# Rows of an expert past 768 as a branched tail of a mixture-of-experts kernel

## The chip, the cores and the metric

The kernel runs on one core of one Trainium2 chip. The metric is the device time of one execution in microseconds (us): median of 3 runs before the change 1105.15 us (1104.6 to 1109.25). The input is drawn with a fixed seed, so each run routes the same tokens to the same experts.

## The reference

```python
x = attn_ref(q, k, v, alpha)        # gated linear attention, (3072 tokens, 384)
logits = x @ w_gate                 # 8 experts
noisy = logits + np.log1p(np.exp(x @ w_noise)) * noise
top2 = np.argpartition(-noisy, 2, axis=1)[:, :2]
w = softmax of the two chosen noisy logits
for e in range(8):                  # tokens that chose e
    h = np.maximum(x[mask] @ w1[e], 0.0)          # 384 -> 1024
    out[mask] += w[mask, k, None] * (h @ w2[e])   # 1024 -> 384
return ((out @ w_a) * (out @ w_b)) @ w_out        # 384 -> 1536 -> 384
```

Each token goes to two experts, so 6144 rows are shared by 8 experts, 768 on average. Counted from the reference on its fixed input, the experts 0 to 7 get 748, 771, 773, 759, 762, 760, 749 and 822 rows.

## The kernel before

TensorE (PE) does everything in full precision by splitting each float32 operand into a high and a low part (`split`, L106) and adding three products (`prod3`, L629 to L631): high by high, high by low, low by high. Each of the three is one weight load (LDWEIGHTS, row PEld) and one matmul (row PE).

The program is written out by hand, in order, engine by engine. After the attention (to about 154 us) the experts follow one another. Expert e has a fixed number of row places: `CAP` = 832 for experts 1 to 6, and `ROWS` = 896 for experts 0 and 7 (`rows_of`). Experts 0 and 7 are "parted": rows of the first 14 token tiles lie in the first `CAPA` = 512 places, the others start at place 512, with a gap between where the first group has fewer. For expert 0 this lets the first part begin before the routing of the last tiles is known, for expert 7 it lets the last layer gather its first rows early. Rows past the capacity set a flag, and a slow path at the end (`tc.If(over > 0)`, L914) computes everything again; on this input it is not taken.

An expert is an up stage and a down stage. In the up stage (`up_unit`), for each of 8 slices f of the hidden dimension, 9 matmuls (3 slices of 384 inputs by 3 products) stream the rows as columns: experts 1 to 6 in two halves of 416 columns, so 8 x 2 x 9 = 144 matmuls; expert 7 in parts of 512 and 384 columns, 72 matmuls each. ScalarE (ACT) and VectorE (DVE) then write the high and low part of the result to `HB` (L646, L647). In the down stage (`down_unit`), each of 7 tiles of 128 rows takes 24 matmuls of 384 columns; the last tile of an expert with 832 places overlaps the tile before it and writes 64 rows. ACT copies the result out (L663), and a DMA puts it into the table `y2` in device memory.

Beside this, ACT and POOL split the next weights (`w_split`, L108, L109), POOL gathers the next expert's rows, PE transposes them (`x_unit`, L370) and ACT and DVE split them (L372, L373). In expert 7, `gather2` fetches rows of `y2` for the last layer, `x2_sum` adds the two experts of a token, and `x2_unit` transposes the sum; `split_more` splits the last layer's weights. In the last layer (`up2_unit`, `down2_unit`) no row count enters.

`nc.values_load` (L816) reads the flag into a register of every engine, after expert 0. The Exp and Ln of the routing (L232, L237, L344) make ACT load function tables in between.

Of the kernel before, what the change touches and what calls it, by code (L numbers as in the profile page):

```python
# [7 lines left out]
F32 = mybir.dt.float32  # L8
# [13 lines left out]
DM = H * D  # L22
KD = DM // 128
E = 8
# [6 lines left out]
CAPA, CAPB = 512, 384  # L31
CAP = 832
ROWS = CAPA + CAPB
NJ = 7
# [13 lines left out]
def parted(e):  # L48
    return e in (0, E - 1)

# [10 lines left out]
def moe_kernel(ctx: ExitStack, tc, qka0, qka1, afirst, v, wgn, noise, w1, w2, w3, out):  # L61
# [14 lines left out]
    xd = tc.dram_tile([N, DM], F32, name="xd")  # L76
    total = base_of(E - 1) + ROWS
    y2 = tc.dram_tile([total, DM], F32, name="y2")
# [19 lines left out]
    idx = tl(const, [128, E * NJ], I32, "idx")  # L98
    flag = tl(const, [1, 1], I32, "flag")

    sctx = ctx.enter_context(ExitStack())
# [76 lines left out]
    def route_consts():  # L178
        nc.sync.dma_start(wgn_t, wgn)
        nc.sync.dma_start(noise_t, noise)  # L180
        iota(e4096, [[4096, E]])
        iota(prio, [[-1, E]], base=E)
        iota(keys.rearrange("p (e j) -> p e j", e=E), [[32, E], [1, NJ]])
        iota(lane, [[1, 128]])
        iota(token, [[128, NT]], base=-1024, channel=1)
        nc.gpsimd.memset(lacc, 1024.0)
        nc.gpsimd.memset(least, 0.0)
        nc.gpsimd.memset(least[:, ::E - 1], CAPA / 128)
        nc.gpsimd.memset(room[:, 0], float(N))
        nc.gpsimd.memset(room[:, 0, ::E - 1], float(CAPA))  # L190
        nc.gpsimd.memset(room[:, 1], float(CAP))
        nc.gpsimd.memset(room[:, 1, ::E - 1], float(ROWS))
        for n, t in d0.items():
            nc.gpsimd.memset(t, 1.0)
            nc.gpsimd.memset(t[:, :, 0:1], 0.0)
# [16 lines left out]
    def route(g):  # L212
# [77 lines left out]
        if half:  # L290
            nc.vector.tensor_tensor(counts[:, int(last)], pc, room[:, int(last)], op=ALU.is_gt)
            if not last:
                carry[0] = tl(rt, [128, E], F32, "carry")
# [39 lines left out]
    def weights():  # L333
# [6 lines left out]
        nc.vector.tensor_tensor(rf, rf, ri, op=ALU.add)  # L340
        nc.vector.tensor_scalar(row[:, :SPLIT], rf[:, :SPLIT], float(total - CAPB - 1), None, op0=ALU.min)
        nc.vector.tensor_scalar(row[:, SPLIT:], rf[:, SPLIT:], float(total - 1), None, op0=ALU.min)
# [292 lines left out]
    def up_unit(e, f, cols):  # L635

        for s0, n in cols:
# [11 lines left out]
            tick()  # L649

    def down_unit(e, j, mid={}):
        c0 = min(128 * j, rows_of(e) - 128)
# [111 lines left out]
    def gather2(i):  # L764
        g = []
        for k in range(2):
            t = tl(rows, [128, DM], F32, "row")
            src = y2[:total - CAPB] if i < SPLIT else y2
            nc.gpsimd.indirect_dma_start(out=t, out_offset=None, in_=src,  # L769
# [38 lines left out]
    for j in range(NA, NJ):  # L808
# [6 lines left out]
        bg()  # L815
    over = nc.values_load(flag[0:1, 0:1], min_val=0, max_val=1)  # L816
    for e in range(1, E - 1):
        for f in range(NF1):
            up_unit(e, f, [(0, CAP // 2), (CAP // 2, CAP // 2)])
            if f < NJ:  # L820
                gather(e + 1, f)
            w_split()
            w_load()
            bg()
        for j in range(NJ):
            x_unit(e + 1, j)
            down_unit(e, j)
            for _ in range(1 + (j == NJ - 1)):
# [9 lines left out]
    for f in range(NF1):  # L838
        up_unit(e, f, parts[0])
        w_split()  # L840
# [7 lines left out]
    for f in range(NF1):  # L848
        up_unit(e, f, parts[1])
        if f < NFREE:  # L850
            split_more()
    for j in range(TB):
        x2_sum(j)
    for j in range(NA, NJ):
        n = j - NA
        down_unit(e, j, {f: (lambda q=q: x2_unit(q)) for f, q in (((5, 0),), ((3, 1),), ((1, 2),))[n]})
        for _ in range(4):
            split_more()


# [148 lines left out]
```

## Time and profile before

| | |
|---|---|
| runs (3) | 1104.6, 1105.15, 1109.25 us |
| profiled execution: own time, span of the trace | 1108.54 us, 1106.8 us |
| PE busy, chain of waits | 97% of the span; 92% of the chain |
| granted TensorE clock, mean | 0.979 |
| expert 1 (up from 228.68, down from 256.18) | to 287.99 us |
| expert 7 | 584.45 to 643.99 us |
| last layer | 643.99 us to the end |

The rows of the trace that matter stand in a section of their own below. "Start" is counted from the start of the span. A matmul's own duration (0.33 us and the like) is longer than the distance between two starts, since matmuls are pipelined: what a stretch costs is read from the distance between starts. DVEq, PEldq and the like are an engine's instruction sequencer, which runs ahead of the engine.

### The profile page before, as it was taken

What the parts mean: (1) busy time and instruction counts of PE and PEld (TensorE: products, weight loads), DVE (VectorE), ACT (ScalarE), POOL (GpSimd) and SP (SyncE); (2) the same over time, 40 slices, a digit from 0 to 9 for tenths busy, and PEclk for the clock granted to TensorE, in tenths of its full rate; (3) what the DMA queues carried; (4) which work ended last, traced back from release to release, by engine and by line L of the source; (5) the groups of instructions that cost most, each with busy time, mean ns of one, the idle gap of its engine ahead of it and who ended that gap; (6) DMA issues with size and microseconds to landing.
All of it is one profiled execution on the core that took longest, in us unless ns stands there. A gap on an engine that the chain in (4) does not pass through costs nothing.

```text
span 1106.8 us, 19015 instructions
## 1 busy us (share of the span) xinstructions
PE 1075.2 (97%) x7482; PEld 1045.3 (94%) x7482; DVE 485.8 (44%) x850; ACT 416.3 (38%) x900; POOL 401.6 (36%) x428
## 2 busy tenths in 40 slices
PE   7997997999999999999999999999999999999998
PEld 5996877899999999999998999999999999999997
DVE  8988847554443536262622364231314141414130
ACT  2454252454444444443533454232323231313131
POOL 5785523475655546473734364010101010100000
PEclk9998598999999999999999999999999999999999
DMA  8999022563544454454523363011111101010000
GB/s 283 241 234 217 32 78 81 172 201 120 161 132 153 146 163 137 132 161 129 187 89 97 108 194 106 23 30 35 30 37 29 36 22 44 22 36 1 22 1 24
DMA packets 62861, 114.71 MB, mean 104 GB/s; under 512 B 8528, under 2 KB 50352, under 8 KB 62768
## 3 DMA queue, kind: packets, MB, share of 16 engines
q1 hardware_dynamic: 56208, 93.59, 28.2%
q0 software_dynamic: 6560, 19.86, 6.2%
q8 instruction: 61, 1.00, 0.4%
q14 instruction: 32, 0.26, 0.1%
HBM read 86.48 MB, written 26.94 MB: 102 GB/s over the span
## 4 chain that ended last, share of the span: by engine, by line
PE 92%; DVE 5%; issue 1%; POOL 1%; ACT 1%; DMA 0%; SPq 0%; DVEq 0%; POOLq 0%; ACTq 0%
PE bank L629 27%; PE bank L630 27%; PE bank L631 27%; PE bank L370 2%; PE bank L484 2%; PE bank L508 2%; PE bank L500 1%; PE bank L476 1%; PE bank L531 1%; DVE D L454 1%; DVE A L458 1%; PE bank L564 1%; PE bank L445 1%; DVE at L315 1%; PE bank L553 0%
## 5 line engine op out<-in xcount | busy, mean ns | idle before, releaser
L629 PE MATMUL bank<-X,W 128*128 128x384 f32 (+2 forms) x768 | 264.4, 344 | 1.5 <-ACT X L372 1.1
L630 PE MATMUL bank<-X,W 128*128 128x384 f32 (+2 forms) x768 | 264.3, 344 | 0.2 <-DVE X L373 0.2
L631 PE MATMUL bank<-X,W 128*128 128x384 f32 (+2 forms) x768 | 264.1, 344 | 0.0
L109 POOL TENSOR_TENSOR W<-wst,W 128x384 fp32r<-128x384 f32 x136 | 139.3, 1028 | 177.3 <-ACT W L108 171.2
L629 PE MATMUL bank<-W,HB 128*128 128x384 f32 x448 | 157.0, 351 | 0.0
L631 PE MATMUL bank<-W,HB 128*128 128x384 f32 x448 | 151.9, 339 | 0.0
L769 POOL DMA_INDIRECT row<-y,row x48 | 46.7, 972 | 289.8 <-DVE row L777 186.1
L630 PE MATMUL bank<-W,HB 128*128 128x384 f32 x448 | 151.8, 339 | 0.0
L629 PEld LDWEIGHTS bank<-X,W 128*128 128x128 f32 x768 | 144.2, 188 | 4.4 <-ACT X L372 1.4
L630 PEld LDWEIGHTS bank<-X,W 128*128 128x128 f32 x768 | 144.2, 188 | 2.9 <-DVE X L373 0.5
L631 PEld LDWEIGHTS bank<-X,W 128*128 128x128 f32 x768 | 144.2, 188 | 2.5
L373 DVE TENSOR_TENSOR X<-bank,X 128x384 fp32r<-128x384 f32 (+1 forms) x80 | 43.2, 542 | 200.6 <-ACT X L372 193.9
L871 DVE TENSOR_TENSOR p<-bank,a 128x384 f32<-128x384 f32 x96 | 53.5, 558 | 162.7 <-PE bank L631 161.6
L647 DVE SCALAR_TENSOR_TENSOR HB<-bank,HB 128x416 fp32r<-128x416 f32 (+2 forms) x128 | 76.3, 597 | 103.3 <-ACT HB L646 98.4
L872 ACT ACTIVATE HB<-p 128x384 fp32r<-128x384 f32 x96 | 50.4, 525 | 156.0 <-DVE p L871 151.5
L646 ACT ACTIVATE HB<-bank 128x416 fp32r<-128x416 f32 (+2 forms) x128 | 67.1, 524 | 95.7 <-PE bank L631 83.9
L663 ACT ACTIVATE o<-bank 128x384 f32<-128x384 f32 (+1 forms) x56 | 27.6, 492 | 156.2 <-PE bank L631 109.5
L629 PEld LDWEIGHTS bank<-W,HB 128*128 128x128 f32 x448 | 84.8, 189 | 0.5
L630 PEld LDWEIGHTS bank<-W,HB 128*128 128x128 f32 x448 | 84.9, 189 | 0.1
L631 PEld LDWEIGHTS bank<-W,HB 128*128 128x128 f32 x448 | 84.6, 189 | 0.0
L629 PE MATMUL bank<-EX,HB 128*128 128x384 f32 x240 | 82.1, 342 | 0.0
L630 PE MATMUL bank<-EX,HB 128*128 128x384 f32 x240 | 80.3, 335 | 0.0
(177 smaller groups left out, 1805.5 us busy)
## 6 DMA issues: line engine op xcount, KB each, us to landing
wst<-w SPq DMA_DIRECT2D x128, 192.0 KB
wd<-w SPq DMA_DIRECT2D x36, 384.0 KB
ring<-qka SPq DMA_DIRECT2D x36, 288.0 KB
y<-o SPq DMA_DIRECT2D x50, 192.0 KB
w3f<-u SPq DMA_DIRECT2D x36, 192.0 KB
wst<-w3f SPq DMA_DIRECT2D x36, 192.0 KB
v<-v SPq DMA_DIRECT2D x24, 192.0 KB
xd<-x SPq DMA_DIRECT2D x24, 192.0 KB
```

The lines of the kernel that those rows point to most:

```text
L109: eng.tensor_tensor(l, raw, h.bitcast(F32), op=ALU.subtract)
L370: nc.tensor.transpose(pt[:, k * 128:k * 128 + m], t[:m, k * 128:k * 128 + 128], ident[:m, :m])
L373: nc.vector.tensor_tensor(l, ptv, h.bitcast(F32), op=ALU.subtract)
L629: nc.tensor.matmul(ps, ah, bh, start=first, stop=False)
L630: nc.tensor.matmul(ps, ah, bl, start=False, stop=False)
L631: nc.tensor.matmul(ps, al, bh, start=False, stop=last)
L646: nc.scalar.activation(Hh[:, f, s], pu, AF.Relu)
L647: nc.vector.scalar_tensor_tensor(Hl[:, f, s], pu, 0.0, Hh[:, f, s].bitcast(F32), op0=ALU.max, op1=ALU.subtract)
L663: nc.scalar.activation(o[r0:], pd[r0:], AF.Copy)
L769: nc.gpsimd.indirect_dma_start(out=t, out_offset=None, in_=src, in_offset=bass.IndirectOffsetOnAxis(ap=row[:, i, k:k + 1], axis=0))
L871: nc.vector.tensor_tensor(p, ps[1], a, op=ALU.mult)
L872: nc.scalar.activation(Ph[:, f], p, AF.Copy)
```

## The change

Experts 1 to 7 now have 832 places each, with no gap in expert 7 (expert 0 keeps 896). Their up stage streams 768 rows in every case. The last 64 places (768 to 831) become a tail: `up_tail` computes all 8 slices f for these 64 columns in one bank (72 matmuls of 64 columns), and `down_tail` is the old seventh tile of the down stage (24 matmuls). Both sit in a branch on PE alone, on whether the expert has more than 768 rows; in the other case PE does one matmul into the same bank, whose result no row uses. ACT and DVE do their part in both cases, and in both cases the 64 rows are written. VectorE computes the eight truth values (`tails`), and PE loads seven of them into registers right after the flag. In expert 7, `x2_unit(2)` moves from the middle of the last down tile to behind it, and `split_more` is called six times after each of two tiles instead of four times after each of three. One table set that holds both Exp and Ln is loaded at the start.

```diff
@@ -30,6 +30,7 @@
 SPLIT = 14
 CAPA, CAPB = 512, 384
 CAP = 832
+MAIN = 768
 ROWS = CAPA + CAPB
 NJ = 7
 GROUPS = (14, 10)
@@ -46,7 +47,7 @@
 
 
 def parted(e):
-    return e in (0, E - 1)
+    return e == 0
 
 
 def rows_of(e):
@@ -74,7 +75,8 @@
         return tl(psum, [128, 512], F32, f"bank{i}")
 
     xd = tc.dram_tile([N, DM], F32, name="xd")
-    total = base_of(E - 1) + ROWS
+    total = base_of(E - 1) + CAP
+    early = base_of(E - 1) + CAPA
     y2 = tc.dram_tile([total, DM], F32, name="y2")
     wide = w3.dtype != F32
     w3f = tc.dram_tile([128, 3 * NF2 * 384], F32, name="w3f") if wide else None
@@ -97,6 +99,8 @@
     wt = tl(const, [128, NT, 2], F32, "wt")
     idx = tl(const, [128, E * NJ], I32, "idx")
     flag = tl(const, [1, 1], I32, "flag")
+    tails = tl(const, [1, E], I32, "tails")
+    nc.scalar.preload_act_table_set("natural_log_exp_and_others")
 
     sctx = ctx.enter_context(ExitStack())
     wpool = sctx.enter_context(tc.tile_pool(name="wpool", bufs=1))
@@ -185,11 +189,11 @@
         iota(token, [[128, NT]], base=-1024, channel=1)
         nc.gpsimd.memset(lacc, 1024.0)
         nc.gpsimd.memset(least, 0.0)
-        nc.gpsimd.memset(least[:, ::E - 1], CAPA / 128)
+        nc.gpsimd.memset(least[:, 0:1], CAPA / 128)
         nc.gpsimd.memset(room[:, 0], float(N))
         nc.gpsimd.memset(room[:, 0, ::E - 1], float(CAPA))
         nc.gpsimd.memset(room[:, 1], float(CAP))
-        nc.gpsimd.memset(room[:, 1, ::E - 1], float(ROWS))
+        nc.gpsimd.memset(room[:, 1, 0:1], float(ROWS))
         for n, t in d0.items():
             nc.gpsimd.memset(t, 1.0)
             nc.gpsimd.memset(t[:, :, 0:1], 0.0)
@@ -289,7 +293,9 @@
         nc.vector.tensor_tensor(rs, pr, e4096[:, None, :].to_broadcast(sh), op=ALU.add)
         if half:
             nc.vector.tensor_tensor(counts[:, int(last)], pc, room[:, int(last)], op=ALU.is_gt)
-            if not last:
+            if last:
+                nc.vector.tensor_scalar(tails, pc[0:1], float(MAIN), None, op0=ALU.is_gt)
+            else:
                 carry[0] = tl(rt, [128, E], F32, "carry")
                 nc.vector.scalar_tensor_tensor(carry[0], pc, 1 / 128, least, op0=ALU.mult, op1=ALU.max)
         for k in range(2):
@@ -338,7 +344,7 @@
         nc.vector.tensor_scalar(e1, ei, 1.0, float(ROWS - CAP), op0=ALU.min, op1=ALU.mult)
         nc.vector.scalar_tensor_tensor(rf, ei, float(CAP), e1, op0=ALU.mult, op1=ALU.add)
         nc.vector.tensor_tensor(rf, rf, ri, op=ALU.add)
-        nc.vector.tensor_scalar(row[:, :SPLIT], rf[:, :SPLIT], float(total - CAPB - 1), None, op0=ALU.min)
+        nc.vector.tensor_scalar(row[:, :SPLIT], rf[:, :SPLIT], float(early - 1), None, op0=ALU.min)
         nc.vector.tensor_scalar(row[:, SPLIT:], rf[:, SPLIT:], float(total - 1), None, op0=ALU.min)
         yield
         nc.scalar.activation(dm, dm, AF.Exp)
@@ -648,6 +654,37 @@
                                            op0=ALU.max, op1=ALU.subtract)
             tick()
 
+    def up_tail(e):
+
+        s = slice(MAIN, CAP)
+        n = CAP - MAIN
+        pu = bank(2 + upn[0] % 4)[:, :NF1 * n]
+        upn[0] += 1
+        with tc.If(more_rows[e] > 0) as c:
+            for f in range(NF1):
+                for k in range(KD):
+                    ks = slice(k * 128, k * 128 + 128)
+                    prod3(pu[:, f * n:f * n + n], (w1h(f)[:, ks], w1l(f)[:, ks]), (Xh[:, k, s], Xl[:, k, s]),
+                          k == 0, k == KD - 1)
+        with c.Else():
+            nc.tensor.matmul(pu, w1h(0)[:, :128], Xh[:, 0, :NF1 * n], start=True, stop=True)
+        pu = pu.rearrange("p (f n) -> p f n", f=NF1)
+        nc.scalar.activation(Hh[:, :, s], pu, AF.Relu)
+        nc.vector.scalar_tensor_tensor(Hl[:, :, s], pu, 0.0, Hh[:, :, s].bitcast(F32), op0=ALU.max, op1=ALU.subtract)
+
+    def down_tail(e):
+        s = slice(CAP - 128, CAP)
+        pd = bank(6 + MAIN // 128 % 2)[:, :DM]
+        with tc.If(more_rows[e] > 0) as c:
+            for f in range(NF1):
+                prod3(pd, (Hh[:, f, s], Hl[:, f, s]), (w2h(f), w2l(f)), f == 0, f == NF1 - 1)
+        with c.Else():
+            nc.tensor.matmul(pd, Hh[:, 0, s], w2h(0), start=True, stop=True)
+        o = tl(outs, [128, DM], F32, "o")
+        r0 = MAIN - (CAP - 128)
+        nc.scalar.activation(o[r0:], pd[r0:], AF.Copy)
+        nc.sync.dma_start(y2[base_of(e) + MAIN:base_of(e) + CAP], o[r0:])
+
     def down_unit(e, j, mid={}):
         c0 = min(128 * j, rows_of(e) - 128)
         s = slice(c0, c0 + 128)
@@ -765,7 +802,7 @@
         g = []
         for k in range(2):
             t = tl(rows, [128, DM], F32, "row")
-            src = y2[:total - CAPB] if i < SPLIT else y2
+            src = y2[:early] if i < SPLIT else y2
             nc.gpsimd.indirect_dma_start(out=t, out_offset=None, in_=src,
                                          in_offset=bass.IndirectOffsetOnAxis(ap=row[:, i, k:k + 1], axis=0))
             g.append(t)
@@ -814,17 +851,23 @@
             w_load()
         bg()
     over = nc.values_load(flag[0:1, 0:1], min_val=0, max_val=1)
+    more_rows = {e: nc.values_load(tails[0:1, e:e + 1], engines=[mybir.EngineType.PE], min_val=0, max_val=1)
+                 for e in range(1, E)}
     for e in range(1, E - 1):
         for f in range(NF1):
-            up_unit(e, f, [(0, CAP // 2), (CAP // 2, CAP // 2)])
+            up_unit(e, f, [(0, MAIN // 2), (MAIN // 2, MAIN // 2)])
             if f < NJ:
                 gather(e + 1, f)
             w_split()
             w_load()
             bg()
+        up_tail(e)
         for j in range(NJ):
             x_unit(e + 1, j)
-            down_unit(e, j)
+            if j < NJ - 1:
+                down_unit(e, j)
+            else:
+                down_tail(e)
             for _ in range(1 + (j == NJ - 1)):
                 w_split()
                 w_load()
@@ -836,7 +879,7 @@
     EX = tl(epool, [128, (NF2 - 2) * 768], F32R, "EX")
     e = E - 1
     for f in range(NF1):
-        up_unit(e, f, parts[0])
+        up_unit(e, f, [(0, CAPA)])
         w_split()
         w_load()
         if f >= NF1 - 4:
@@ -846,16 +889,19 @@
     for j in range(TB):
         gather2(j)
     for f in range(NF1):
-        up_unit(e, f, parts[1])
+        up_unit(e, f, [(CAPA, MAIN - CAPA)])
         if f < NFREE:
             split_more()
+    up_tail(e)
     for j in range(TB):
         x2_sum(j)
-    for j in range(NA, NJ):
+    for j in range(NA, NJ - 1):
         n = j - NA
-        down_unit(e, j, {f: (lambda q=q: x2_unit(q)) for f, q in (((5, 0),), ((3, 1),), ((1, 2),))[n]})
-        for _ in range(4):
+        down_unit(e, j, {f: (lambda q=q: x2_unit(q)) for f, q in ((), ((1, 0), (5, 1)))[n]})
+        for _ in range(6):
             split_more()
+    down_tail(e)
+    x2_unit(2)
 
 
     def up2_unit(blk, f):
```

TensorE's order before, behind expert 0's last down tile (the names: `W` the split weights, `HB` the hidden rows, `X` the transposed rows, `bank` a PSUM bank; the number at the end is partitions by columns):

```order
L629 MATMUL bank_610_3028<-W_86,HB_2324 128x384
L630 MATMUL bank_610_3028<-W_86,HB_2324 128x384
L631 MATMUL bank_610_3028<-W_86,HB_2324 128x384
L816 TENSOR_LOAD flag_82
L629 MATMUL bank_620_3099<-X_93,W_86 128x416
L630 MATMUL bank_620_3099<-X_93,W_86 128x416
L631 MATMUL bank_620_3099<-X_93,W_86 128x416
```

and now:

```order
L635 MATMUL bank_611_3031<-W_88,HB_2326 128x384
L636 MATMUL bank_611_3031<-W_88,HB_2326 128x384
L637 MATMUL bank_611_3031<-W_88,HB_2326 128x384
L853 TENSOR_LOAD flag_82
L854 TENSOR_LOAD tails_83
L854 ISA x2
...
L635 MATMUL bank_621_3172<-X_95,W_88 128x384
L636 MATMUL bank_621_3172<-X_95,W_88 128x384
L637 MATMUL bank_621_3172<-X_95,W_88 128x384
```

Between the flag's load and the first matmul of expert 1 stand now seven loads of a truth value (the pair of `tails` rows above, seven times), each followed by two register instructions (ISA), and the first matmul has 384 columns instead of 416.

TensorE's order now, around the tail of expert 1's up stage (before, the transposes L370 followed the last matmul of 416 columns at once):

```order
L635 MATMUL bank_660_3428<-X_95,W_88 128x384
L636 MATMUL bank_660_3428<-X_95,W_88 128x384
L637 MATMUL bank_660_3428<-X_95,W_88 128x384
L663 COMPARE_AND_BRANCH
L635 MATMUL bank_663_3449<-X_95,W_88 128x64
L636 MATMUL bank_663_3449<-X_95,W_88 128x64
L637 MATMUL bank_663_3449<-X_95,W_88 128x64
...
L663 UNCONDITIONAL_BRANCH
L670 MATMUL bank_663_3449<-X_95,W_88 128x512
L663 UNCONDITIONAL_BRANCH
L376 MATMUL bank_664_3526<-ident_70,row_3196 128x128 x3
L635 MATMUL bank_665_3532<-W_88,HB_2326 128x384
```

Behind the compare-and-branch stand the 72 matmuls of 64 columns (three shown), a jump over the other case, the one matmul of the other case, and a jump to the transposes of the next expert's first tile. `down_tail` has the same form with 24 matmuls of 384 columns (L678, L682).

TensorE's order now, at the end of expert 7:

```order
L637 MATMUL bank_1181_7661<-W_88,HB_2326 128x384
L678 COMPARE_AND_BRANCH
L635 MATMUL bank_1191_7725<-W_88,HB_2326 128x384
L636 MATMUL bank_1191_7725<-W_88,HB_2326 128x384
L637 MATMUL bank_1191_7725<-W_88,HB_2326 128x384
...
L678 UNCONDITIONAL_BRANCH
L682 MATMUL bank_1191_7725<-W_88,HB_2326 128x384
L678 UNCONDITIONAL_BRANCH
L376 MATMUL bank_1193_7755<-ident_70,row_7404 128x128 x3
L635 MATMUL bank_1194_7761<-X_95,W_88 128x384
L636 MATMUL bank_1194_7761<-X_95,W_88 128x384
```

The transposes of the third tile of the last layer's first block (L376) now stand right before that layer's first matmul, which reads what ACT and DVE make of them; before, they stood between matmuls of the last down tile.

## Rows read from the trace of the kernel before

**Rows 1.** Page, busy time of the engines: share of the span, instructions.

```profile
PE 1075.2 (97%) x7482; PEld 1045.3 (94%) x7482; DVE 485.8 (44%) x850; ACT 416.3 (38%) x900; POOL 401.6 (36%) x428
```

**Rows 2.** Page, chain of waits that ended last, share by engine.

```profile
PE 92%; DVE 5%; issue 1%; POOL 1%; ACT 1%; DMA 0%; SPq 0%; DVEq 0%; POOLq 0%; ACTq 0%
```

**Rows 3.** Timeline of TensorE, starts of expert 1: up, transposes, down (start, duration).

```profile
228.68 0.35 PE L629 MATMUL bank<-X,W 128*128 128x416 f32 x1
...
255.93 0.49 PE L370 MATMUL bank<-ident,row 128*128 128x128 f32 x3
256.18 0.42 PE L629 MATMUL bank<-W,HB 128*128 128x384 f32 x1
```

**Rows 4.** Timeline of TensorE, starts of the parts of expert 7.

```profile
584.45 0.39 PE L629 MATMUL bank<-X,W 128*128 128x512 f32 x1
...
600.81 0.35 PE L629 MATMUL bank<-W,HB 128*128 128x384 f32 x1
...
617.71 0.34 PE L629 MATMUL bank<-X,W 128*128 128x384 f32 x1
...
630.20 0.34 PE L629 MATMUL bank<-W,HB 128*128 128x384 f32 x1
```

**Rows 5.** Timeline of TensorE weight loads behind a transpose.

```profile
216.36 0.19 PEld L629 LDWEIGHTS bank<-W,HB 128*128 128x128 f32 x1
216.47 0.19 PEld L630 LDWEIGHTS bank<-W,HB 128*128 128x128 f32 x1
```

**Rows 6.** Chain of waits in the attention (start, length, what).

```profile
86.06 0.87 PE bank L500 x8
...
88.02 1.07 PE bank L508 x32
```

**Rows 7.** Line L816, the flag: duration min/median/max in ns, start.

```profile
L816 PEldq TENSOR_LOAD <-flag x1: 492/492/492, 226.2 to 226.2; - x1
...
L816 SPq TENSOR_LOAD <-flag x1: 498/498/498, 231.2 to 231.2; - x1
L816 SPq FUSED_REGOPS  x1: 191/191/191, 231.8 to 231.8; - x1
L816 SPq SEQ_ASSERT  x1: 29/29/29, 232.0 to 232.0; - x1
```

**Rows 8.** Timeline of TensorE around its longest idle time near expert 0.

```profile
186.55 0.20 PE L327 MATMUL bank<-bt,at 128*128 128x56 f16 x1 [4.60 <-DVE bt L320]
...
188.10 0.52 PE L631 MATMUL bank<-W,HB 128*128 128x384 f32 x1
...
190.02 0.52 PE L631 MATMUL bank<-W,HB 128*128 128x384 f32 x1
```

**Rows 9.** Stretches: length, busy us of PE, PEld, DVE, ACT, POOL; PE clock, DMA.

```profile
9.60:101.70 92.10, 85.00 (x1590) 77.38 (x1589) 80.49 (x124) 43.88 (x100) 68.10 (x78) 1.00 1.00 250
...
183.60:190.50 6.90, 3.79 (x20) 3.79 (x21) 5.95 (x19) 0.45 (x2) 4.46 (x4) 0.51 0.16 53
...
228.70:256.20 27.50, 27.50 (x149) 27.15 (x147) 19.18 (x27) 15.32 (x34) 21.75 (x22) 1.00 0.60 194
```

**Rows 10.** Line L914, the branch on the flag.

```profile
L914 DVEq COMPARE_BRANCH  x1: 72/72/72, 1084.1 to 1084.1; - x1
...
L914 PEldq COMPARE_BRANCH  x1: 3641/3641/3641, 1098.2 to 1098.2; - x1
```

**Rows 11.** Timeline of TensorE, its last matmul.

```profile
1101.17 0.34 PE L631 MATMUL bank<-HB 128*128 128x384 f32 x1
```

**Rows 12.** Page, DMA queues: packets, MB, share.

```profile
q8 instruction: 61, 1.00, 0.4%
```

**Rows 13.** Timeline: TensorE waits for transposed rows.

```profile
200.41 0.45 PE L629 MATMUL bank<-X,W 128*128 128x384 f32 x1 [1.09 <-ACT X L372]
```

**Rows 14.** Timeline of ACT behind a down tile of expert 7.

```profile
640.07 1.75 ACT L108 ACTIVATE W<-wst 128x384 fp32r<-128x384 f32 x4
```

**Rows 15.** Groups by line: table loads of the Ln.

```profile
L237 ACT ACT_TABLE_LOAD x2 | 2.6, 1283 | 0.0
```

## What the change should do to the time

> **What bounds the kernel now.** I read the busy times first, then the chain of waits, then the timeline of TensorE. PE is busy 97% of the span and no other engine over 44% [rows 1]; the chain that ended last is PE for 92% and DVE for 5% [rows 2]. The DVE part lies in the attention and in the routing before 187 us; in the experts PE has no gap at all: in expert 1's up stage it is busy 27.50 of 27.50 us, with ACT at 15.3 and POOL at 21.8 [rows 9]. So a PE instruction taken away there is won in full, one added is lost in full, and the other engines matter only where PE comes to wait for them. The forecast is therefore a count of matmuls times the distance between their starts.
>
> That distance depends on the columns. 416 columns: expert 1's up stage starts at 228.68, and the transposes behind its 144 matmuls at 255.93, so 27.25 / 144 = 0.189 us [rows 3]. 512 columns: (600.81 - 584.45) / 72 = 0.227. 384 columns: (630.20 - 617.71) / 72 = 0.1735. A down tile of 24 matmuls: (617.71 - 600.81) / 4 = 4.22 us, 0.176 each [rows 4].
>
> **The parts.** Which side of the branch is taken follows from the counts in the reference: of experts 1 to 7, three are over 768 (771, 773 and 822), four are not.
>
> 1. Up stage of experts 1 to 6 with 768 columns: 6 x 144 x (0.189 - 0.1735) = -13.6 us.
>
> 2. Four experts skip the tail. Each loses a down tile of 4.22 us and gains one matmul of 512 and one of 384 columns, 0.227 + 0.176: 4 x -3.82 = -15.3 us.
>
> 3. Three experts pay for the up tail: 3 x 72 matmuls of 64 columns, while their down tail costs what the seventh tile did. No matmul of the split operands has so few columns in this trace. From 512 to 384 columns the distance falls by 0.42 ns a column, which would give 0.04 us at 64, but the weights (128 columns) must be loaded for each. Two weight loads of this kind with no long matmul between them start 0.11 us apart [rows 5], and in the attention eight matmuls with 128 weight columns and 96 moving ones take 0.87 us, 0.109 each [rows 6]. Below: 32 loads of 64 weight columns, two side by side, take 1.07 us, so 128 columns in 0.067. Above: what 384 columns cost, 0.1735. A tail is thus 4.8 to 12.5 us; I take 0.109, by the loads of the same kind: 7.85 us, and 3 x 7.85 = +23.5 us (14.5 to 37.5).
>
> 4. Expert 7's second part has 256 columns instead of 384. By 0.42 ns a column that is 0.119 us, still above a weight load: 72 x (0.119 - 0.1735) = -3.9 us (0 at the least, -4.6 if only the load counts).
>
> 5. Seven register loads on PE. The flag's load ran in PE's sequencer at 226.2 for 492 ns, and the matmul behind it started at 228.68: the sequencer is 2.5 us ahead [rows 3, 7]. Of a load with its two register instructions SP shows the whole: load at 231.2, operation at 231.8, assertion at 232.0 [rows 7], 0.85 us from one to the next. Seven are 6.0 us, behind the flag's 0.55, so the first matmul of expert 1 can start at 226.2 + 6.55 + 0.1 = 232.85 instead of 228.68: +4.2 us. Bounds: 0 if loads overlap one another enough, 6.0 if the sequencer's lead is gone when it arrives. Behind them waits all of PE, and so ACT and DVE with the results of expert 1.
> The Trainium skill, page "Runtime: NRT & Kernel Launch", section "Instruction fetch mechanics", puts such a load at about 200 ns a register; this trace shows 467 to 547 on its engines, and the measurement decides. By the page's figure the stall would be an estimated 2 us.
>
> 6. The clock after that stall. PE's one idle time of this length near here, 4.60 us before 186.55 [rows 8], left the granted clock at 0.51 for 183.6 to 190.5 [rows 9], that is at 1.2 GHz: six matmuls of 384 columns from 188.10 to 190.02, 0.32 each, instead of 0.176. From 187.3 to 190.4, when the clock was back, some ten ran that way: 10 x 0.144 = +1.4 us (0 to 3).
>
> 7. The end of expert 7. The third tile's transposes now run with nothing behind them but the matmul that needs them. Such a wait stands in the trace: 1.09 us [rows 13]. Ahead of it ACT has six weight splits instead of four; four took 1.75 us [rows 14], so six take 2.6, within the 4.2 us of the down tail if their data has arrived. I take +1.5 us (1.1 to 3).
>
> 8. The branches. On DVE a taken jump cost 72 ns [rows 10]; PE's sequencer is 2.5 us ahead and hides that. 0, but see the rival.
>
> 9. Table loads of 1283 ns [rows 15]: four of five vanish from the middle, but ACT is 38% busy and has 1% of the chain [rows 1, 2]: 0 (to -1.3). `tails` is one DVE instruction more in the routing, which PE waits for: +0.2 us.
>
> The sum: -13.6 - 15.3 + 23.5 - 3.9 + 4.2 + 1.4 + 1.5 + 0.2 = -2.0 us. The profiled execution took 1108.54 us (span 1106.8), 3.4 above the median of the runs; from its own time that gives 1106.5, and by the median, which I predict, 1105.15 - 2.0 = 1103 us. Half a per cent, 5.5 us, is about what a measurement of this kernel tells from no change.
>
> **Rivals.**
>
> A. Every branch on PE costs a fetch of its code (the slower side). PE's own jump over the slow path took 3641 ns, not 72 [rows 10]. It began at 1098.2, while the last matmul queued before it started at 1101.17 [rows 11] and a next one could have started at 1101.34; the jump ended at 1101.9, so a stall of 0.6 us was left. For it: fourteen compare-and-branches, and in the skipping case a second jump after a single matmul, with nothing queued to hide it. Against it: code comes in packets of 1.00 MB / 61 = 16 KB [rows 12] for about 15,000 PE instructions, so some 250 each; the slow path is longer than two of these, while the longest new jump passes 72 matmuls with their loads, 144 instructions, and lands in the present packet or the next. Price: at least 14 x 0.6 = +8.4 us, 1111.5; with the second jump of the four skipping experts' branches at 3.6 each, 8 x 3.6 = 29 more, 1140. It decides from 0.55 us a branch.
> The Trainium skill, same page and section, says that a taken branch whose target is outside the two-page window waits for its page to be fetched. The 3641 ns agree; no run yet shows a jump of 144 instructions.
>
> B. The tails run dear: at the distance of 384 columns, 37.5 us instead of 23.5, 1117; or the clock falls in them, where the ratio 0.32 / 0.176 makes them 43 us, 1122. Against it: the attention's small matmuls kept a granted clock of 1.00 for 92 us [rows 9].
>
> C. The register loads cost nothing, because they overlap, and so the clock does not fall: -5.6, 1097.5. Against it: the operation behind each load needs its value, and SP started it only after the load's end.
>
> D. The tails run cheap, 0.067 a matmul: 3 x 72 x 0.042 = -9.1, 1094.
>
> E. The change does not split as counted: 771 and 773 are near 768, and each expert that changes sides is worth 7.85 + 4.22 - 0.4 = 11.7 us. Counts that stand three and five away need more than rounding, so this is small; both skipping would give 1079.5.
>
> **How the numbers follow.** Forecast 0.47, with its own range 1098 to 1110 from the smaller bounds of steps 4 to 9; A 0.16, B 0.12, C 0.12, D 0.10, E 0.03. Faster by over 0.5% (under 1099.6) are C, D and E: 0.25. Slower by over 0.5% (over 1110.7) are A and B: 0.28. The same: 0.47. The range that leaves out no more than 2 in 10 goes from D's 1094 to 1114, which takes in A's lower price and leaves out its upper one, most of B, and E.
>
> **What would show it.** In the profile after: the up stage of expert 3 lasts near 25.0 us and its down stage near 27.8 (steps 1, 2); 72 matmuls of 64 columns in three experts, 0.109 us apart (step 3, against B and D), and none in four (E); 256 columns 0.119 apart (step 4); PE idle some 4 us before expert 1's first matmul, with eight loads in its sequencer, and the clock at 0.5 behind it (steps 5, 6, against C); 1 to 3 us idle before the last layer's first matmul (step 7); PE's COMPARE_BRANCH rows near 0.1 us (against 3.6 for A). The forecast is wrong if the tails are off by 0.03 us a matmul, if a branch costs over 0.55 us, or if an engine other than PE begins to stop it in the shortened experts, where POOL's share rises from 79% of the up stage to 87%.

## The result and the profile after

The changed kernel took 1124.06 us, the median of 4 runs (1120.98 to 1125.76); the kernel before took 1107.2 us in 4 runs beside them (1104.6 to 1110.56). The ratio is 1.0147, with a 95% interval of 1.0107 to 1.0188: slower by 17 us. The forecast was 1103 us, within 1094 to 1114, so both its side and its range were wrong. Rival B in its second form (the clock falls in the tails, 1122) is what happened.

The page of the kernel after, busy time, the granted clock in 40 slices, and the chain by engine, beside [rows 1, 2]:

```profile
PE 1081.1 (96%) x7610; PEld 1053.0 (94%) x7610; DVE 469.4 (42%) x858; ACT 412.0 (37%) x903; POOL 404.6 (36%) x428
...
PEclk9999698988998999999999899999999999999999
...
PE 85%; DVE 6%; DMA 4%; issue 3%; ACT 1%; POOL 1%; SPq 0%; POOLq 0%; ACTq 0%; DVEq 0%
```

PE is busy as before, but for longer. The mean granted clock is 0.965, against 0.979 before. Next, the timeline of TensorE after: where expert 1's up stage, its tail, its down stage and expert 2 start, then the same for expert 3, which skips its tail, and expert 7's part of 256 columns and its tail; beside [rows 3, 4].

```profile
234.50 0.68 PE L635 MATMUL bank<-X,W 128*128 128x384 f32 x1 [3.03 <-ACT rf L772]
...
262.32 0.19 PE L635 MATMUL bank<-X,W 128*128 128x64 f32 x1
...
273.06 0.67 PE L635 MATMUL bank<-W,HB 128*128 128x384 f32 x1
...
307.15 0.33 PE L635 MATMUL bank<-X,W 128*128 128x384 f32 x1
...
401.98 0.39 PE L670 MATMUL bank<-X,W 128*128 128x512 f32 x1
...
402.46 0.42 PE L635 MATMUL bank<-W,HB 128*128 128x384 f32 x1
...
430.25 0.34 PE L635 MATMUL bank<-X,W 128*128 128x384 f32 x1
...
625.09 0.28 PE L635 MATMUL bank<-X,W 128*128 128x256 f32 x1
...
633.72 0.20 PE L635 MATMUL bank<-X,W 128*128 128x64 f32 x1
```

Expert 1 lasts 307.15 - 234.50 = 72.65 us instead of 59.31. Its up stage takes 27.82, 10.2 us go by from the first matmul of the tail to the transposes, and the down stage takes 34.1 instead of 31.8. Expert 3's down stage takes 430.25 - 402.46 = 27.79. The same timeline, inside the tail of expert 1:

```profile
267.59 0.28 PE L635 MATMUL bank<-X,W 128*128 128x64 f32 x1
267.70 0.29 PE L636 MATMUL bank<-X,W 128*128 128x64 f32 x1
267.81 0.40 PE L637 MATMUL bank<-X,W 128*128 128x64 f32 x1
268.02 0.40 PE L635 MATMUL bank<-X,W 128*128 128x64 f32 x1
268.24 0.40 PE L636 MATMUL bank<-X,W 128*128 128x64 f32 x1
```

Up to 267.81 the starts are 0.11 us apart, behind it 0.21. The stretches of the kernel after say why (length, busy us of PE, PEld, DVE, ACT and POOL, the granted clock, DMA share, GB/s): expert 1's up stage, its tail up to that point and behind it, and the tails of experts 2 and 7.

```profile
234.50:262.30 27.80, 27.80 (x144) 27.80 (x145) 14.18 (x25) 12.63 (x28) 19.11 (x19) 0.89 0.51 158
262.30:267.80 5.50, 5.50 (x52) 5.50 (x51) 0.78 (x2) 1.31 (x3) 2.95 (x3) 1.00 0.22 80
267.80:272.50 4.70, 4.70 (x24) 4.70 (x23) 0.00 (x0) 0.00 (x0) 0.00 (x0) 0.50 0.00 0
332.10:344.20 12.10, 12.10 (x76) 12.10 (x76) 0.76 (x2) 1.60 (x4) 2.95 (x3) 0.67 0.10 39
633.70:643.30 9.60, 9.60 (x74) 9.60 (x73) 0.43 (x1) 0.38 (x1) 4.80 (x5) 0.82 0.38 113
```

The granted clock is 1.00 in the first part of the tail and 0.50, that is 1.2 GHz, in the second, and PE is busy in all of both. The busy columns show nothing of this fall: the clock column and the distance between starts do.

The loads of the truth values (line, sequencer, count, min/median/max in ns, first and last start), then the branches of `up_tail` (seven compares, and in the three experts with a tail a jump over the other case) and that over the slow path, beside [rows 7, 10]:

```profile
L854 PEldq TENSOR_LOAD <-tails x7: 299/306/532, 229.4 to 233.8; - x7
L854 PEldq FUSED_REGOPS  x7: 146/146/160, 229.8 to 234.2; - x7
```

```profile
L663 PEldq COMPARE_BRANCH  x10: 65/188/343, 259.2 to 639.7; - x10
```

```profile
L960 PEldq COMPARE_BRANCH  x1: 3497/3497/3497, 1115.3 to 1115.3; - x1
```

The loads follow one another (233.8 - 229.4) / 6 = 0.73 us apart, and PE stands for 3.03 us at 234.50. The timeline names ACT for that wait; but PE's own sequencer was in these loads until 234.4. The new branches take a tenth of the long one at most, and PE has no idle time behind them.

TensorE's wait after, at the end of expert 7, and the chain of waits there (start, length, what):

```profile
660.63 0.44 PE L635 MATMUL bank<-X,W 128*128 128x384 f32 x1 [1.91 <-ACT X L378]
```

```profile
654.75 0.39 ACT o L700
655.16 0.32 SPq L701
655.58 0.37 SPq L117
656.05 2.96 DMA wst<-w3f
659.03 0.53 ACT X L112
659.57 0.48 ACT o L685
660.08 0.50 ACT X L378
660.61 0.57 DVE X L379
661.22 0.45 PE bank L636
```

The last layer's matmul waited (1.91 us at 660.63, then 0.3 more at 661.22) not for the transposes but for what stood ahead of their copy on ACT: a weight split whose data landed at 659.01, because SP had issued its DMA only behind the write of the down tile's rows.

By stage, from one profiled execution to the other (1108.54 to 1125.76, +17.2): up to the start of expert 0 +4.8, expert 0 with the loads +1.0, expert 1 +13.3, expert 2 +10.6, experts 3 to 6 -22.3, expert 7 +9.2, the rest +0.6.

### The profile page after: what moved, and what is told of

Same layout as the page of the kernel before. It is cut to its first block, busy times and chain, and to the rows that moved or that the text cites. A ratio compares the mean times of both kernels' runs of the same rounds, so it can differ in the third digit from the quotient of the medians.

```text
span 1124.0 us, 19331 instructions
## 1 busy us (share of the span) xinstructions
PE 1081.1 (96%) x7610; PEld 1053.0 (94%) x7610; DVE 469.4 (42%) x858; ACT 412.0 (37%) x903; POOL 404.6 (36%) x428
## 4 chain that ended last, share of the span: by engine, by line
PE 85%; DVE 6%; DMA 4%; issue 3%; ACT 1%; POOL 1%; SPq 0%; POOLq 0%; ACTq 0%; DVEq 0%
PE bank L635 25%; PE bank L636 25%; PE bank L637 25%; PE bank L376 2%; PE bank L490 2%; PE bank L514 2%; DMA wd<-w 1%; DMA wst<-w 1%; PE bank L506 1%; PE bank L482 1%; DMA ring<-qka 1%; DVE D L460 1%; PE bank L537 1%; DVE A L464 1%; DVE at L321 1%
## 5 line engine op out<-in xcount | busy, mean ns | idle before, releaser
L635 PE MATMUL bank<-X,W 128*128 128x384 f32 (+3 forms) x840 | 282.5, 336 | 6.4 <-ACT rf L772 3.0
L636 PE MATMUL bank<-X,W 128*128 128x384 f32 (+3 forms) x840 | 282.3, 336 | 0.1
L637 PE MATMUL bank<-X,W 128*128 128x384 f32 (+3 forms) x840 | 282.2, 336 | 0.0
L635 PEld LDWEIGHTS bank<-X,W 128*128 128x128 f32 x840 | 162.3, 193 | 9.9 <-ACT rf L772 3.3
L636 PEld LDWEIGHTS bank<-X,W 128*128 128x128 f32 x840 | 162.4, 193 | 2.5 <-DVE X L379 0.7
L637 PEld LDWEIGHTS bank<-X,W 128*128 128x128 f32 x840 | 162.5, 193 | 1.9
L635 PE MATMUL bank<-W,HB 128*128 128x384 f32 x416 | 148.4, 357 | 0.0
L636 PE MATMUL bank<-W,HB 128*128 128x384 f32 x416 | 143.1, 344 | 0.0
L637 PE MATMUL bank<-W,HB 128*128 128x384 f32 x416 | 143.0, 344 | 0.0
L653 DVE SCALAR_TENSOR_TENSOR HB<-bank,HB 128x384 fp32r<-128x384 f32 (+2 forms) x128 | 71.2, 563 | 90.3 <-ACT HB L652 86.6
L652 ACT ACTIVATE HB<-bank 128x384 fp32r<-128x384 f32 (+2 forms) x128 | 62.8, 496 | 78.1 <-PE bank L637 77.7
L635 PE MATMUL bank<-EX,HB 128*128 128x384 f32 x240 | 82.0, 342 | 0.0
L635 PEld LDWEIGHTS bank<-W,HB 128*128 128x128 f32 x416 | 80.8, 194 | 0.3
L636 PEld LDWEIGHTS bank<-W,HB 128*128 128x128 f32 x416 | 80.6, 194 | 0.1
L637 PE MATMUL bank<-EX,HB 128*128 128x384 f32 x240 | 80.3, 334 | 0.0
L636 PE MATMUL bank<-EX,HB 128*128 128x384 f32 x240 | 80.3, 334 | 0.0
L637 PEld LDWEIGHTS bank<-W,HB 128*128 128x128 f32 x416 | 80.1, 193 | 0.0
```

The lines of the kernel that those rows point to most:

```text
L635: nc.tensor.matmul(ps, ah, bh, start=first, stop=False)
L636: nc.tensor.matmul(ps, ah, bl, start=False, stop=False)
L637: nc.tensor.matmul(ps, al, bh, start=False, stop=last)
L652: nc.scalar.activation(Hh[:, f, s], pu, AF.Relu)
L653: nc.vector.scalar_tensor_tensor(Hl[:, f, s], pu, 0.0, Hh[:, f, s].bitcast(F32), op0=ALU.max, op1=ALU.subtract)
```

## The experiments

Runs of a group shared a chip and the runs of the kernel before, whose median was 1107.01 us for the first four, 1112.58 for the next four and 1105.01 for the last two. They are compared by their ratio to it; 1% is 11 us.

**First group: what the tails, the loads and the tables are worth.**

No expert takes its tail (`e1_never`); the rows past 768 of experts 1, 2 and 7 are left out of the result:

```diff
-    nc.vector.tensor_scalar(tails, pc[0:1], float(MAIN), None, op0=ALU.is_gt)
+    nc.vector.tensor_scalar(tails, pc[0:1], 4096.0, None, op0=ALU.is_gt)
```

> The changed kernel with the threshold of the tails at 4096, so that all seven experts skip: rows past 768 of experts 1, 2 and 7 are left out. Theory (a tail costs its 72 matmuls of 64 columns at 0.111 us, its down tile, and a fall of the clock that outlasts it): experts 1, 2 and 7 lose 16.4, 16.3 and 14.9 us, the time falls by some 47 us to about 1077, and the granted clock has no 0.5 stretch near the ends of the up stages. Rival (most of the added 17 us lies outside the tails, in the attention, the loads and the end of expert 7): a tail is then worth 7.9 + 4.2 us, the time falls by 36 us to about 1088.

Measured: 1081.43 us, 0.9768 [0.9735, 0.9801], between the two. From 257 to 598 us, behind expert 1's up stage, the clock is 1.00 throughout. Against the changed kernel that is 42 us less; three tails at full clock with their down tiles are 3 x 11.7 = 35, and the clock lost in them is 13 more (below). Of the 6 us that are missing from 48, most was lost again at the end of expert 7, as the timeline of this run shows:

```profile
609.44 0.55 PE L376 MATMUL bank<-ident,row 128*128 128x128 f32 x3 [1.69 <-DVE X L379]
614.71 0.69 PE L635 MATMUL bank<-X,W 128*128 128x384 f32 x1 [4.72 <-ACT X L378]
```

Without the tail's matmuls PE waits 6.4 us there, 4.2 more than in the changed kernel. Another 2 us went in the up stages of experts 2 and 3, which now follow a skipped tail: 25.95 and 26.12 us instead of 24.96.

Tails of 192 columns, of which only the last 64 are used (`e2_wide192`), in four banks:

```diff
+    w = 192
+    sw = slice(CAP - w, CAP)
...
-                    prod3(pu[...], (w1h(f)[:, ks], w1l(f)[:, ks]), (Xh[:, k, s], Xl[:, k, s]), ...)
+                    prod3(pu, (w1h(f)[:, ks], w1l(f)[:, ks]), (Xh[:, k, sw], Xl[:, k, sw]), ...)
...
-            nc.tensor.matmul(pu, w1h(0)[:, :128], Xh[:, 0, :NF1 * n], start=True, stop=True)
+            for pu in pus:
+                nc.tensor.matmul(pu, w1h(0)[:, :128], Xh[:, 0, :2 * w], start=True, stop=True)
```

> The changed kernel with 192 columns (places 640 to 831) instead of 64 in each of the 72 matmuls of a tail, of which the last 64 are used as before; a skipping expert does four matmuls of 384 columns instead of one of 512. Theory (the clock falls because the tail's matmuls are so short; the distance between starts is that of the weight load): the distance stays near 0.111 us, the clock stays at 2.4 GHz through the tails, and the time falls by some 12 us less 2 for the skipping experts, to about 1114. Rival (the clock falls for another reason, as the branch or the wait for banks, or the distance grows with the columns): the time stays at 1124 or rises by 2.

Measured: 1115.23 us, 1.0062 [1.0038, 1.0087], some 9 us less than the changed kernel, for three times the columns. The stretch of the tail of expert 1 in this run:

```profile
260.00:268.20 8.20, 8.20 (x75) 8.20 (x75) 0.77 (x3) 1.63 (x5) 2.99 (x3) 1.00 0.13 51
```

The clock stays at 1.00, here and in the tails of experts 2 and 7. The 72 matmuls take 8.02 us up to the transposes, 0.111 each, the same distance as 64 columns have at full clock, and the down stage behind them is back at 31.8. So the 64 columns were not dear by their number; what they cost beyond that was the clock.

The loads of the truth values one at a time, in the up stage of each expert (`e3_spread`):

```diff
-    more_rows = {e: nc.values_load(...) for e in range(1, E)}
...
+            if f == 4:
+                load_rows(e)
```

> The changed kernel with each of the seven register loads moved into its own expert's up stage, behind slice 4, instead of all seven ahead of expert 1. Theory (the sequencer's lead of 2.5 us hides one load of 0.7 us, and the fall of the clock behind the stall goes with the stall): no idle time of 3.0 us ahead of expert 1, no clock of 0.5 there, time lower by 5.9 us, about 1118. Rival (the clock falls there anyway, or each load stalls PE a little): lower by 3 us at most, 1121 or more.

Measured: 1119.7 us, 1.0108 [1.0079, 1.0137], 4.4 us less. Expert 1's up stage starts with no idle time and takes 24.99 us at a clock of 1.00:

```profile
228.80:253.70 24.90, 24.90 (x145) 24.90 (x145) 15.56 (x27) 14.85 (x33) 22.11 (x22) 1.00 0.64 204
```

The tails still lose the clock; that of expert 7 takes 12.55 us in this execution. The interval (1115.8 to 1122.2 us) holds the theory's 1118 and the rival's 1121 alike; that the stall and the low clock behind it are gone is shown by the trace, not by the time.

The kernel before with only the table set at the start (`e4_before_table`):

```diff
+    nc.scalar.preload_act_table_set("natural_log_exp_and_others")
```

> The kernel before with the one table set loaded at the start, and nothing else of the change. In the profile of the changed kernel the attention ended 4.8 us later than before. Theory (that is the attention's DMA, which differs from execution to execution): same time as before, 1107, and the start of expert 0 lies between 154 and 159 us without relation to the tables. Rival (the one table set slows the attention): 1112 us, expert 0 starts near 159.

Measured: 1107.22 us, 1.0000 [0.9977, 1.0022]: the tables are worth nothing that can be told, within 2.5 us. The start of expert 0 lay at 154.39 us before, 159.17 after, 152.72 here, and at 159.87 and 157.91 in two runs below that have the tables and the attention of the kernel before (`e7_dummy`, `e9_between`). So the 4.8 us between the two first profiles are not the change's: the attention varies by that much from one execution to another. Without them the stages give +12.4, which lies in the interval of the ratio (11.8 to 20.8 us), near its lower end.

**Second group: what makes the clock fall, and repairs.**

The operands of the up tail exchanged (`e5_swap`): the 64 rows are the weights, and 18 matmuls stream 512 hidden columns each; eight transposes turn the result:

```diff
-                    prod3(pu[...], (w1h(f)[:, ks], w1l(f)[:, ks]), (Xh[:, k, s], Xl[:, k, s]), ...)
+                    prod3(pu, (Xh[:, k, s], Xl[:, k, s]), (wh[:, k, fs], wl[:, k, fs]), k == 0, k == KD - 1)
...
+            nc.tensor.transpose(pt[...], t[f // 2][...], ident[:n, :n])
```

> The changed kernel with the operands of the up tail exchanged: the 64 rows are the weights and 512 columns of w1 stream, 18 matmuls instead of 72, then 8 transposes of 64 columns after the third down tile; a skipping expert does 2 matmuls of 512 columns and the transposes. Theory (short matmuls cost the tail by the weight load's distance and by the clock): a tail takes 18 x 0.227 + 0.5 = 4.6 us instead of 10.2, 11.6 and 9.6, the clock stays at 2.4 GHz in and after it (another 4.9 us), the skipping experts pay 0.5 us each: lower by 20.5 us, about 1103.5, as fast as the kernel before within what can be told. Rival (a branched tail makes the clock fall or PE wait whatever its matmuls are): above 1110.

Measured: 1111.28 us beside 1112.58 for the kernel before, 0.9992 [0.9967, 1.0018], so 17 us less than the changed kernel. Two of its tails (the first stretch takes in the transposes behind it):

```profile
266.70:271.10 4.40, 4.40 (x22) 2.64 (x21) 0.79 (x2) 1.57 (x4) 3.01 (x3) 1.00 0.27 96
...
627.30:631.40 4.10, 4.10 (x20) 2.44 (x18) 0.71 (x2) 0.80 (x3) 3.77 (x4) 1.00 0.58 168
```

The 18 matmuls take 4.14 us at a clock of 1.00, and the eight transposes make the down stage 0.85 us longer (32.91 us for 32.06). The three tails gain the clock's 13 us and 3 x (7.85 - 4.99) = 8.6; the four skipping experts pay a second matmul, 0.23 us, and the same transposes, 0.82 us of the down stage (28.86 for 28.04), 4.2 together: 17 by the trace and by the ratios, where the theory had 20.5.

The exchange, the spread loads, and at the end of expert 7 the third tile's transposes back inside the last full down tile, with three of the twelve splits behind the tail (`e6_all`; of its edit, the end of expert 7):

```diff
+        if n:
+            flip_tail(t)
-        down_unit(e, j, {... ((1, 0), (5, 1)))[n]})
-        for _ in range(6):
+        down_unit(e, j, {... ((1, 0), (3, 1), (5, 2)))[n]})
+        for _ in range((6, 3)[n]):
             split_more()
     down_tail(e)
-    x2_unit(2)
+    for _ in range(3):
+        split_more()
```

> The exchanged tail, the register loads spread over the experts, and at the end of expert 7 the third tile's transposes within the down tile ahead of the tail, with three of the weight splits behind it. Theory (three separate losses, which add up): 1103.5 less 4.4 for the loads and 2.5 for the end of expert 7, about 1097, faster than before by 0.9%. Rival (what remains is hidden or limited by ACT and the DMA, as where ACT waits for the last layer's data in the up stages): 1102 or more.

Measured: 1108.46 us, 0.9961 [0.9936, 0.9986]: faster than before by 0.4%, where the theory had 0.9. PE's wait and its chain at the end of expert 7:

```profile
631.35 0.55 PE L376 MATMUL bank<-ident,row 128*128 128x128 f32 x3 [3.20 <-DVE HB L687]
```

```profile
625.48 0.32 SPq L715
625.90 2.76 DMA wst<-w3f
628.68 0.52 ACT W L112
629.21 0.53 ACT W L112
629.76 0.93 DVE W L113
630.69 0.61 DVE HB L687
631.35 0.55 PE bank L376 x3
```

The wait had only moved: the fifth and sixth split behind one tile find no data, and now hold up the transposed tail instead of the last layer; PE stood for 3.20 us.

The kernel before with 72 matmuls of 64 columns behind the up stages of experts 1, 2 and 4, results unused, no branch (`e7_dummy`):

```diff
+        if e in (1, 2, 4):
+            short(e)
```

> The kernel before, with 72 matmuls of 64 columns behind the up stages of experts 1, 2 and 4, into a bank that nothing reads, and no branch. Theory (such a run of matmuls takes 8.0 us and makes the clock fall by itself): each adds 8.0 us and some 4 for the clock, 36 us in all, 1143, with a clock of 0.5 in and behind each. Rival (the branch or the tail's results make the clock fall): 24 us, 1131, clock 1.00.

Measured: 1154.8 us, 1.036 [1.0323, 1.0396], +40 us for what would be 23.5 at full clock. Expert 1's tail in this run, up to the fall, behind it, and the start of the down stage:

```profile
261.30:266.80 5.50, 5.50 (x51) 5.50 (x51) 0.72 (x2) 1.34 (x3) 2.96 (x3) 1.00 0.20 65
266.80:272.00 5.20, 5.20 (x27) 5.20 (x27) 0.00 (x0) 0.00 (x0) 0.00 (x0) 0.50 0.01 3
272.00:277.00 5.00, 5.00 (x18) 5.00 (x17) 1.29 (x3) 0.49 (x1) 0.00 (x0) 0.50 0.00 0
```

The same fall with no branch, no register load and none of the other edits; and 5 us of the down stage's long matmuls are paid at half clock as well before it rises.

The changed kernel with only the end of expert 7 altered (`e8_endfix`):

```diff
-        for _ in range(6):
+        for _ in range((6, 3)[n]):
```

together with the third tile's transposes back inside the last full tile, and three splits behind the tail.

> The changed kernel with only the end of expert 7 altered: the third tile's transposes within the down tile ahead of the tail, three of the twelve weight splits behind the tail. Theory (PE stands 1.9 us and a further 0.5 there because ACT is behind splits that wait for their data): lower by 2.5 us, 1121.5. Rival (the last layer's first matmuls then wait for the splits instead): same as the changed kernel, 1124.

Measured: 1131.45 us, 1.0154 [1.012, 1.0187], against 1.0147: no gain that can be told. The wait has only moved to the transposes, behind the same late `wst` transfer, which landed at 657.53; six splits still follow one tile:

```profile
660.09 0.55 PE L376 MATMUL bank<-ident,row 128*128 128x128 f32 x3 [2.42 <-DVE X L379]
```

**Third group: the form of the fall, and the late transfer.**

The 3 x 72 short matmuls of `e7_dummy`, nine at a time between the slices (`e9_between`):

```diff
             up_unit(e, f, [(0, CAP // 2), (CAP // 2, CAP // 2)])
+            if e in (1, 2, 4):
+                short(e, f)
```

> The kernel before with the same 3 x 72 matmuls of 64 columns as in the run with 72 in a row behind the up stages of experts 1, 2 and 4, but nine at a time, behind each slice of the up stage; no branch, the results are not used. If it is the long stretch of nothing but short matmuls that lets the clock fall, the clock stays at 1.00 here and the nine cost 9 x 0.109 = 0.98 us a slice: 24 x 0.98 = +23.5 us, a ratio of 1.021 to 1.022. If short matmuls cost the clock wherever they stand, it is again about +40 us, 1.036. Signs: no phase at 0.5 between 205 and 600 us and up stages of 35.1 us in the first case.

Measured: 1130.17 us, 1.0212 [1.0165, 1.0259], +23 us. Up and down stage of expert 1 in this run:

```profile
230.30:265.70 35.40, 35.40 (x219) 35.12 (x218) 19.03 (x28) 16.45 (x36) 22.02 (x22) 1.00 0.49 157
265.80:297.50 31.70, 31.70 (x188) 31.21 (x187) 7.53 (x17) 10.87 (x26) 13.03 (x13) 1.00 0.35 112
```

The same instructions cost 17 us less than in a row, and the clock stays at 1.00 from 205 to 600 us: it is the long row of short matmuls that does it, not their number.

`e6_all` with four splits behind each of the last three tiles, as before the change (`e10_four`):

```diff
-        for _ in range((6, 3)[n]):
+        for _ in range(4):
             split_more()
     down_tail(e)
-    for _ in range(3):
+    for _ in range(4):
```

> The run with all three repairs, with one thing put back as it was before the change: in expert 7, four weight splits behind each of the last three down tiles instead of six, three and three. In that run PE stood idle for 3.20 us at 631.35, behind a DVE split that waited for ACT, which waited to 628.68 for the data of its fifth and sixth weight split; the DMA for these had been issued only at 625.90, behind the write of the tile's rows on SP. If that is the chain, the gap goes and so does the low clock behind it (3.4 us at 0.5, some 1.2 us): -4 us against that run, ratio to the kernel before about 0.9925 instead of 0.9961. If the wait was for DVE or for the transposes in any case, the ratio stays at 0.996.

Measured: 1098.0 us (1095.3 to 1100.93, 9 runs), 0.9925 [0.9898, 0.9953], the fastest that computes all rows. What is left of the wait:

```profile
623.29 0.55 PE L376 MATMUL bank<-ident,row 128*128 128x128 f32 x3 [1.18 <-DVE HB L687]
```

The number of splits between two down tiles, which no one counts as work of PE, was worth 4 us by the ratios. Their intervals overlap; the trace is the firmer sign: the gap of 3.20 us shrinks to 1.18, and from the end of its up tail to the last layer expert 7 takes 15.88 us instead of 19.47.

## Why the prediction was wrong

**Step 1** (768 columns) was right: an up stage at full clock takes 24.96 us, forecast 25.0. **Step 2** (four skip) was right in its own size, a down stage of 27.79 us for 27.8, but experts 3 to 6 gained 22.3 instead of 24.3: the up stages of experts 4 to 6, each behind a skipped tail, take 25.46, 25.87 and 25.46 us. They show waits that the longer stages had covered, such as this in expert 5, where a split by DVE came late after ACT had waited 2.33 us for a transfer of `wd`:

```profile
491.02 0.44 PE L635 MATMUL bank<-X,W 128*128 128x384 f32 x1 [0.63 <-DVE HB L653]
```

The prediction named such a wait as a way to fail (it looked to POOL) and priced it at nothing.

**Step 3 failed.** It priced a tail at 72 x 0.109 = 7.85 us. The distance was right, 0.11 us, as long as the clock was full. The clock was what it had taken as given: the fall costs 4.9 us in expert 1 (2.6 in the tail, 2.3 in the down stage behind it), 5.0 in expert 2 and 3.1 in expert 7, 13.0 together, worked out from the stages against 7.85 us and the down stage of before. `e7_dummy` shows it with nothing else changed, `e2_wide192`, `e5_swap` and `e9_between` take it away in three ways. How much runs at half clock differs from one execution to the next: the same three tails took 10.1, 11.5 and 12.6 us in the profile of `e3_spread` and 11.1, 12.6 and 12.7 in that of `e8_endfix`, against 10.2, 11.6 and 9.6 here, and by the same working the clock cost some 16 and 18 us there. So 13 is its size in one execution, the smallest of the three. This may be why the stages without the attention give 12.4 us and the medians 16.9, which is not shown. The argument against rival B was the attention's clock of 1.00 for 92 us [rows 9]. That was a row on another mixture of work: there the short matmuls stand in runs of 8 and 32 [rows 6] of several shapes, and PE is idle for 7.1 of the 92.1 us. And it was only a part of what the trace of before shows of this mixture; the stretch right behind it, columns as in [rows 9], speaks for the rival:

```profile
101.70:139.30 37.60, 32.57 (x322) 29.67 (x324) 30.93 (x59) 9.21 (x20) 19.81 (x21) 0.50 0.24 66
```

There the clock had fallen behind idle time of PE, and then matmuls of the same lines of the kernel ran at 0.50 to the end of the stretch, with PE busy for 30.94 of the last 33.10 us: a busy PE was no warrant for the full clock. Why the mixture keeps a full clock, and 72 alike in a row lose it, no run here settles.

Rival B named the right cause, but that its 1122 came so near is partly luck: it put the whole tail at half clock (43 us for three), while the mean clock of 0.67 and 0.82 in the tails of experts 2 and 7 says that about two thirds and one third of these ran so, and the rest was paid in the down stage.

**Step 4** was right: 256 columns took 8.63 us, 0.120 each, forecast 0.119.

**Steps 5 and 6** were right together and wrong apart; that the two errors cancel is luck. The stall was 3.03 us, not 4.2: PE's own loads take 306 ns at the median, not the 498 of SP's from which the step was worked out [rows 7], and follow one another 0.73 us apart instead of 0.85. The clock behind it cost 27.82 - 24.96 = 2.9 us, not 1.4; in the profiles of `e5_swap` and `e8_endfix`, with the same seven loads, it cost 1.7 (26.63 us). Together 5.9, forecast 5.6; `e3_spread` gave back 4.4. Two short waits of PE in expert 0 (0.70 and 1.09 us [rows 13 for the second]) did not occur in this execution, which is why that stage shows only +1.0; the prediction's "no gap at all" in the experts holds from expert 1 on. Rival C (the loads overlap) is refuted: each load is followed by its register operation, and then by the next.
The Trainium skill, page "Runtime: NRT & Kernel Launch", section "Instruction fetch mechanics", puts a register load at about 200 ns; by the page's table of terms that is a load from device memory. Here `tails` lies on the chip; PE's loads took 299 to 532 ns, and what counts, a load with its register instructions, 0.73 us.

**Step 7** was right in kind, +1.5 forecast, 2.2 of waits measured, but it named the wrong cause: not the transposes' own latency but the splits ahead of their copy on ACT, whose data had not arrived. "If their data has arrived" was the condition, and the step did not look at what issues that data: SP, behind the write of each tile. In the changed kernel this is read from the chain of waits; `e10_four` shows it by experiment in the repaired one, and `e8_endfix`, which left six splits together, gained nothing.

**Step 8** was right, and **rival A** is refuted: the new compare-and-branches took 65 to 343 ns in a sequencer that is ahead, while the jump over the slow path again took 3497. The Trainium skill, same page and section, says that a taken branch whose target lies outside the fetched window waits for its code. The trace agrees, with 217 to 343 ns for the four jumps over 144 instructions and 3497 over the slow path. **Step 9** was right as to the tables (`e4_before_table`); its 0.2 us for `tails` is too small to be told. **Rival D** (0.067 a matmul) is refuted by the 0.11, and **rival E** by the tails in experts 1, 2 and 7 alone.

The sum of -2.0 against +17.2: the clock in the tails +13.0, attention by chance +4.8, steps 5 and 6 in expert 1 +1.5, the shortened experts +2.0, the end of expert 7 +0.7, the rest +0.6, and expert 0 -3.4 (forecast 4.4, seen 1.0). These are differences between two single executions; between the medians it is 16.9.

## What to carry to other kernels

A tail of few columns should be priced at both clock levels unless a row shows the same kind of run of the same length; one shows nothing for the other. Of the two operands of a thin product, try the thin one as the weights: here that made 18 matmuls of 72, and the clock stayed. After work is removed from the bounding engine, follow each instruction queue in front of the results it then waits for, down to who issues the data: here six splits in place of four were worth as much as one of the named steps.

## What the runs showed of the hardware

The granted clock of TensorE fell to 0.50 while the engine was busy 5.50 of 5.50 us before the fall and all the time behind it; in [rows 8, 9] it had followed idle time. In the attention of the kernel before it stayed at 0.50 for 33.10 us in which the engine was busy for 30.94. Of rows of 72 matmuls at the same distance of 0.111 us, those with 64 columns lost the clock, in all twelve rows of four traces (the changed kernel, `e3_spread`, `e7_dummy`, `e8_endfix`), and those with 192 kept it, in three rows of one; nine of 64 columns between 18 of 416 kept it too. Long matmuls that came behind the fall ran at half clock for 2.6 to 5.8 us more. At full clock the distance was 0.111 us with 64 columns and with 192, 0.120 with 256 and 0.1735 with 384.
